# Attention wave 0 and its expert product: another order of casts, masks and products

## The chip, the cores and the metric

One core of one Trainium2 chip runs the whole program. The metric is the device time of one execution in microseconds. The engines named below are TensorE (PE, with its weight loads PEld), VectorE (DVE), ScalarE (ACT), GpSimd (POOL) and the DMA queue of SyncE (SP). Each works through its own instructions in the order in which they were written; they wait for each other only at semaphores.

## The reference

Linear attention with a decay per head, in blocks of 64 rows, and behind it an MLP on all tokens:

```python
# q, k, v: (4, 8, 768, 64) f32;  lam: (8,);  w_in: (512, 2048);  w_out: (2048, 512)
for b in range(nb):
    intra = einsum('bhic,bhjc->bhij', qb, kb) * Dmask
    intra = einsum('bhij,bhjd->bhid', intra, vb)
    inter = einsum('bhid,bhde->bhie', qb * lam_pow, kv_state)
    out[:, :, sl] = intra + inter
    kv_state = lam_block * kv_state + einsum('bhsd,bhse->bhde', kb * rev_pow, vb)
x = out.transpose(0, 2, 1, 3).reshape(3072, 512)
h = x @ w_in
y = (h / (1 + exp(-1.702 * h))) @ w_out
```

## The kernel before

The 768 rows of the four batches are cut into six waves (`w`) of 512 tokens; the MLP of a wave is done with its attention. Waves 0 and 1 (`w < ND`) take the first 256 rows of one batch as a chunk (`c` = 0, 1; wave 0 has batches 0 and 1, wave 1 has 2 and 3), with two neighbouring rows in one partition; waves 2 to 5 take 128 rows of all four batches. This case is about wave 0 and the beginning of wave 1.

Attention of one chunk in these waves:

- `load_one` brings k, q, v as f32 from DRAM (SP's queue; v of chunk 1 from POOL's queue). `do_cast` (lines 193 to 204) multiplies k or q by powers of the decay and writes bf16: for each half `g` of the heads two instructions of 128x256. Chunk 0's casts are on DVE, k of chunk 1 on POOL, q of chunk 1 on DVE.
- `turn_pe` (line 232) transposes the cast tile on PE into PSUM, and ACT or DVE copies it out (`kT`, `qT`). `cast_v` makes v bf16 (`v_sb`).
- `d_scores` (line 251) makes the scores in PSUM tiles `ps_s`, four tiles for a chunk in two calls, and multiplies each by the mask into `sm`: on DVE from PSUM, or, with `split`, every second tile by an ACT copy to SBUF and a DVE multiplication in place.
- `d_one`/`d_state` make the state `ps_kv` from the cast k and v, `d_keep` copies it out, `d_inter` multiplies q by the state, `d_out` multiplies `sm` by v into `ps_o`, and `d_x` copies that into `xT`, the MLP's input.
- `fill` issues matmuls on zeros into a bank that nobody reads.

The MLP's first product is `mlp1_half` (8 matmuls of 256 columns into one bank, then the GELU on ACT, line 416) and `mlp1` (4 of 512 columns, line 404). The weights come from POOL's queue: `load_w_in` in five chunks, the second of which holds the feature tiles 2 to 4, then `load_w_out` in four. Two DMAs are held back behind others by a tiny instruction that reads a tile: `gate_pool` and `gate_sync`.

The second product (`product`, line 448) is done by seven products of half size with sums of blocks (in the way of Strassen and Winograd), 16 matmuls of 256 columns each. The sums of w_out's blocks are `weight_sums` (steps `W`), those of the MLP's activations `g_sums` (steps `g`), both on DVE; sums of w_in's blocks, which later waves use, are `in_sums` (steps `I`). A bank in PSUM collects several products: by `CHAIN`, products 1, 6, 5 and 3 go to bank X, 2 to Q, 7 and 4 to V. `after_product` (line 471) takes a bank out after each product: ACT copies 1, 6 and 7 to `part`, and DVE adds a `part` to the bank to give a block of the output, `o_sb`, which SP stores; the block of product 2 is held back until step `o`.

The order is written by hand (`manual_schedule`, from line 639): calls for the start, then strings of steps, in which `p1a` is product 1 with the first part of its matmuls (`a`, `b`, `l`, `h` are parts), `P50` is product 5 for its first 128 tokens, `P51` for the second. Between the steps of wave 0 stand the pieces of wave 1's attention (`start`, `end`).

## Time and profile before

| | us |
|---|---|
| runs, median of 3 (lowest, highest) | 192.32 (192.29, 193.49) |
| the profiled execution | 192.84 |
| its span in the trace | 191.1 |
| steady part of a later wave, from one `ps_hX` group to the same one in the next wave (81.16 to 109.20) | 28.04 |

The profile's page gives the busy time of each engine, the chain of work that ended last and the costliest groups; the trace answers for single tiles and stretches. Two more rows are of use for the start: POOL's k casts of chunk 1 wait for the loads, and DVE is idle for 1.21 us before it copies the last `qT` of chunk 0 out.

```profile
9.07 0.42 DVE L218 COPY qT<-ps_t 128x512 bf16<-128x512 bf16 x1 [1.21 <-PE ps_t L238]
11.02 0.81 POOL L181 DMA_DIRECT2D w_in<-in_moe_w_in_dram  x1
16.02 0.43 DVE L267 TENSOR_TENSOR sm<-sm,mask_d 128x512 bf16<-128x512 bf16 x1
16.40 0.59 ACT L265 CAST sm<-ps_s 128x512 bf16<-128x512 f32 x1
```

A row is: start and length in us, engine, line, operation, what it writes and reads, the shapes, how many; in brackets the engine's idle time ahead of it and what ended it. Before the change the copy by ACT and the mask in place occur in chunk 1 of wave 0 alone.

### The profile page before, as it was taken

How to read it: one execution, taken by the hardware profiler on the slowest of the kernel's cores; microseconds unless marked ns; L12 is line 12 of the kernel's file. 1: busy time of each engine (PE TensorE's matmuls, PEld its weight loads, DVE VectorE, ACT ScalarE, POOL GpSimd, SP SyncE). 2: the span in 40 equal slices, each digit the busy share in tenths (PEclk: the TensorE clock that was granted, in tenths of full speed). 3: DMA queues.
4: the chain of work that ended last, by engine and by line, in shares of the span. 5: the costliest groups of instructions: out<-in, count | busy, mean ns of one | idle time of the engine just before them, and what ended most of it. 6: DMA issues, size and time to landing. Idle time of an engine off the chain costs nothing.

```text
span 191.1 us, 5544 instructions
## 1 busy us (share of the span) xinstructions
PE 184.6 (97%) x2297; PEld 152.2 (80%) x2297; DVE 156.3 (82%) x292; ACT 129.6 (68%) x242; POOL 53.7 (28%) x76
## 2 busy tenths in 40 slices
PE   7979999999999999999999999999999999999993
PEld 2557646888888888888888888888888888888882
DVE  1796699979978799879799879799789797888950
ACT  4948665257666986388896288885488876597611
POOL 5499000076495000195000294000492000000000
PEclk9999999999999999999999999999999999999999
DMA  4999999999997997868999555899565903300113
GB/s 144 313 290 197 204 200 209 321 310 229 215 241 178 214 247 165 207 163 139 208 243 216 187 153 127 197 241 230 175 152 122 209 4 113 110 3 0 54 59 110
DMA packets 89599, 33.91 MB, mean 177 GB/s; under 512 B 67430, under 2 KB 89446, under 8 KB 89574
## 3 DMA queue, kind: packets, MB, share of 16 engines
q1 hardware_dynamic: 84676, 28.84, 60.1%
q0 software_dynamic: 4896, 4.72, 14.5%
q8 instruction: 18, 0.29, 0.6%
q14 instruction: 7, 0.06, 0.1%
q10 hardware_dynamic: 2, 0.00, 0.0%
HBM read 27.26 MB, written 6.29 MB: 176 GB/s over the span
## 4 chain that ended last, share of the span: by engine, by line
PE 73%; DMA 11%; DVE 8%; POOL 2%; ACT 2%; issue 1%; SPq 0%; ACTq 0%
PE ps_X L461 19%; PE ps_hX L544 16%; PE ps_V L461 9%; PE ps_hV L544 8%; PE ps_Q L461 5%; DMA w_in<-in_moe_w_in_dram 5%; PE ps_hQ L544 4%; DVE w_in_t L520 3%; DMA kf<-in_k_dram 3%; DMA vf<-in_v_dram 3%; PE ps_h L414 2%; PE ps_s L335 2%; PE ps_o L390 2%; PE ps_fill L147 2%; POOL ks L202 1%; DVE sm L267 1%
## 5 line engine op out<-in xcount | busy, mean ns | idle before, releaser
L461 PEld LDWEIGHTS <-g_s 128*128 128x128 bf16 x384 | 37.0, 98 | 5.0
L563 ACT ACTIVATE g_sb<-h_sb 128x512 bf16<-128x512 f32 x54 | 32.6, 631 | 1.2 <-DVE h_sb L552 1.2
L544 PEld LDWEIGHTS <-w_in_t 128*128 128x128 bf16 x288 | 28.1, 98 | 3.4
L461 PEld LDWEIGHTS <-g_sb 128*128 128x128 bf16 x288 | 27.4, 98 | 4.1
L221 ACT COPY part<-ps_hX 128x512 f32<-128x512 f32 x32 | 18.3, 586 | 11.5 <-PE ps_hX L544 11.5
L461 PE MATMUL ps_X<-w_out_t,g_s 128*128 128x256 bf16 x192 | 23.1, 273 | 0.0
L544 PEld LDWEIGHTS <-w_in 128*128 128x128 bf16 x216 | 21.1, 98 | 2.5
L544 PE MATMUL ps_hX<-x_s,w_in_t 128*128 128x256 bf16 x144 | 21.6, 272 | 0.0
L441 DVE TENSOR_TENSOR g_s<-g_sb 128x1024 bf16<-128x1024 bf16 x24 | 16.3, 687 | 5.9 <-ACT g_sb L563 5.6
L634 POOL CAST behind_q<-x_s 1x1 f32<-1x1 bf16 x3 | 0.5, 174 | 60.3 <-DVE x_s L529 60.3
L209 POOL TENSOR_TENSOR qs<-qf,q_pow 128x512 bf16<-128x512 f32 x16 | 16.6, 1063 | 2.9 <-DMA qf<-in_q_dram 2.9
L209 POOL TENSOR_TENSOR ks<-kf,k_pow 128x512 bf16<-128x512 f32 x16 | 16.8, 1075 | 1.8 <-DMA kf<-in_k_dram 1.8
L474 ACT COPY part<-ps_X 128x512 f32<-128x512 f32 (+1 forms) x14 | 7.3, 522 | 13.0 <-PE ps_X L461 13.0
L218 DVE COPY part<-ps_hV 128x512 f32<-128x512 f32 x18 | 12.4, 688 | 3.7 <-PE ps_hV L544 3.7
L552 DVE TENSOR_TENSOR h_sb<-part,ps_hX 128x512 f32<-128x512 f32 x18 | 12.3, 681 | 2.7 <-PE ps_hX L544 2.7
L552 DVE TENSOR_TENSOR h_sb<-part,ps_hV 128x512 f32<-128x512 f32 x18 | 12.3, 684 | 1.0 <-PE ps_hV L544 1.0
L461 PE MATMUL ps_X<-w_out,g_sb 128*128 128x256 bf16 x96 | 12.6, 273 | 0.0
L461 PE MATMUL ps_Q<-w_out,g_sb 128*128 128x256 bf16 x96 | 12.5, 273 | 0.0
L552 DVE TENSOR_TENSOR h_sb<-part,ps_hQ 128x512 f32<-128x512 f32 x18 | 12.2, 679 | 0.0
L461 PE MATMUL ps_V<-w_out_t,g_sb 128*128 128x256 bf16 x96 | 12.0, 273 | 0.0
L563 ACT ACTIVATE g_sb<-ps_hX 128x512 bf16<-128x512 f32 x18 | 10.6, 588 | 1.8 <-PE ps_hX L544 1.8
L461 PE MATMUL ps_V<-w_out_t,g_s 128*128 128x256 bf16 x96 | 11.6, 273 | 0.0
(111 smaller groups left out, 362.3 us busy)
## 6 DMA issues: line engine op xcount, KB each, us to landing
kf<-in_k_dram SPq DMA_DIRECT2D x10, 512.0 KB, 6.4
qf<-in_q_dram SPq DMA_DIRECT2D x10, 512.0 KB, 7.2
vf<-in_v_dram SPq DMA_DIRECT2D x10, 512.0 KB, 6.0
out_dram<-o_sb SPq DMA_DIRECT2D x24, 128.0 KB, 2.4
out_dram<-o_sb SPq DMA_DIRECT2D x12, 256.0 KB, 2.7
w_out<-in_moe_w_out_dram POOLq DMA_DIRECT2D x4, 512.0 KB, 14.1
kf<-in_k_dram SPq DMA_DIRECT2D x4, 256.0 KB, 3.1
qf<-in_q_dram SPq DMA_DIRECT2D x4, 256.0 KB, 5.2
```

What stands on the lines that cost most here:

```text
L147: nc.tensor.matmul(fill_ps[0], zero[:, 0:P], zero, start=True, stop=True)
L209: eng.tensor_tensor(x.rearrange("p b (r i j d) -> p j (b r) i d", i=2, j=2, d=D)[:, j], f.rearrange("p h (a d) -> p (h a) d", a=2).rearran ...
L218: nc.vector.tensor_copy(out, in_)
L221: nc.scalar.copy(out, in_)
L335: nc.tensor.matmul(s2[h][:, b, :], kT[hs, (b % 2) * NP + p, :], qT[hs, (b % 2) * NP + p, :], start=True, stop=True)
L441: nc.vector.tensor_tensor(o, x, y, op=f)
L461: nc.tensor.matmul(bank[:, t], x[:, m, t * P : (t + 1) * P], y, start=(n in (1, 2, 7) and t == ts[0] * last and m == 0), stop=(m == FFC // ...
L474: nc.scalar.copy(part[w, n, t.start][:, t], bank[:, t])
L520: nc.vector.tensor_tensor(o, x, y, op=SUB)
L544: nc.tensor.matmul(bank[:, u], z[:, kc], y[:, kc], start=(n in (1, 2, 7) and u + kc == 0), stop=(kc == 1), skip_group_check=True)
L552: nc.vector.tensor_tensor(h, h_part[w, g, {2: 1, 5: 7, 4: 6}[n]], bank, op=ADD)
L563: nc.scalar.activation(g_of[w][:, a : b + 1 : b - a, 256 * i : 256 * i + 256], bank, GELU)
```

## The change

In wave 0 and the beginning of wave 1:

- `load_w_in(1)` is issued from POOL's queue ahead of the k casts of chunk 1 instead of between their halves.
- `do_cast` writes a tile in another layout, `[P, NP, 2, P]`, and does a half in one instruction of 128x512. `turn_pe` and `d_state` read that layout.
- The masks leave `d_scores` for `d_masks`. In wave 0, chunks 0 and 1, the two score calls come first, then the masks of the first tile of each call on DVE, then those of the second tiles by an ACT copy and DVE in place.
- Two `fill` matmuls are left out. The transposes of chunk 1, the second state product and the `xT` copies stand in another order, one transposed half is copied out by ACT instead of DVE, and `cast_v(0, 1)` stands behind `mlp1_half(0, 0, 0)` instead of ahead of it.
- In wave 0's second product, product 4 has a bank of its own (Z) and stands in part between 7 and the last parts of 1, 2 and 7. DVE adds product 6 to product 7's `part`; product 5 is copied out by ACT into a `part`, and its sum for the output comes with a new step `u`. Product 3 comes earlier, directly behind product 5 and `d_even`. `start` is now `scores`, `d_one`, `d_keep` and `d_even` at places of their own.

```diff
     def do_cast(w, c, nm, eng, g=None):
         if g in (None, 0):
-            cast[w, c, nm] = work.tile([P, 2, HD], bf16, tag=f"{nm}s{c}", bufs={"k": 2, "q": 1}[nm], name=f"{nm}s")
+            cast[w, c, nm] = work.tile([P, NP, 2, P] if w < ND else [P, 2, HD], bf16, tag=f"{nm}s{c}",
+                                       bufs={"k": 2, "q": 1}[nm], name=f"{nm}s")
...
-                for j in range(2):
-                    h = slice(4 * R + 2 * j, 4 * R + 2 * j + 2)
-                    eng.tensor_tensor(x.rearrange("p a (r i j d) -> p r j i a d", i=2, j=2, d=D)[:, R, j],
-                                      f[:, h].rearrange("p i (a d) -> p i a d", a=2),
-                                      pw[:, h].unsqueeze(3).to_broadcast([P, 2, 2, D]), op=MUL)
+                h = slice(4 * R, 4 * R + 4)
+                eng.tensor_tensor(x[:, 2 * R : 2 * R + 2].rearrange("p i a (j d) -> p j (i a) d", j=2),
+                                  f[:, h].rearrange("p (j i) (a d) -> p j (i a) d", j=2, a=2),
+                                  pw[:, h].rearrange("p (j i) a -> p j (i a)", j=2).unsqueeze(3).to_broadcast([P, 2, 4, D]),
+                                  op=MUL)
...
-        for h in range(2):
+        masked[w, c, pp] = s2
+
+    def d_masks(w, c, pp, hh=(0, 1), split=()):
+        for h in hh:
             sm = work.tile([P, 2, 2, P], bf16, tag="sm", bufs=8, name="sm")
-            flat = s2[h].rearrange("p (i a) s -> p i (a s)", i=2)
-            if split and h:
+            flat = masked[w, c, pp][h].rearrange("p (i a) s -> p i (a s)", i=2)
+            if h in split:
                 nc.scalar.copy(sm.rearrange("p i a s -> p i (a s)"), flat)
...
+        own = w == 0 and n == 4
+        if own and ms[0] == 0:
+            blocks[w, "Z", key] = acc("ps_Z", shape=[P, 2, 256])
+        bank = blocks[w, "Z" if own else CHAIN[n], key]
...
         if n in (1, 6, 7):
             part[w, n, t.start] = op.tile([P, 2, 256], f32, tag="part", bufs=6, name="part")
-            nc.scalar.copy(part[w, n, t.start][:, t], bank[:, t])
+            if n == 6 and w == 0:
+                nc.vector.tensor_tensor(part[w, n, 0], part[w, 7, 0], bank, op=ADD)
+            else:
+                nc.scalar.copy(part[w, n, t.start][:, t], bank[:, t])
...
+        if n == 5 and w == 0 and (w, 5) not in part:
+            part[w, 5] = op.tile([P, 2, 256], f32, tag="part", bufs=6, name="part")
+            nc.scalar.copy(part[w, 5], bank)
+            c22[w] = partial(after_product, w, n, part[w, 5], t)
+            return
...
         load_one(0, 1, "v", v)
+        load_w_in(1)
         cast_v(0, 0, (act_copy, act_copy))
         d_scores(0, 0, 0)
         d_scores(0, 0, 1)
-        fill(3)
+        for h in range(2):
+            for pp in range(2):
+                d_masks(0, 0, pp, (h,), (1,))
+        fill(2)
         do_cast(0, 1, "k", nc.gpsimd, 0)
-        load_w_in(1)
         do_cast(0, 1, "k", nc.gpsimd, 1)
...
-        d_state(0, 0, states[0, 0], Z)
         do_cast(0, 1, "q", nc.vector, 0)
         do_cast(0, 1, "q", nc.vector, 1)
-        d_x(0, 0, 0, oa, act_copy)
+        turn_pe(0, 1, "k", act_copy, 1)
         turn_pe(0, 1, "q", act_copy, 0)
         d_inter(0, 0, oz, 0, False)
-        turn_pe(0, 1, "k", dve_copy, 1)
         turn_pe(0, 1, "q", dve_copy, 1)
+        d_state(0, 0, states[0, 0], Z)
+        d_x(0, 0, 0, oa, act_copy)
         d_x(0, 0, 1, oz, act_copy)
-        fill(1, "a")
-        d_scores(0, 1, 0, True)
+        d_scores(0, 1, 0)
+        d_scores(0, 1, 1)
+        for h in range(2):
+            for pp in range(2):
+                d_masks(0, 1, pp, (h,), (1,))
+        mlp1_half(0, 0, 0)
         cast_v(0, 1, (act_copy, dve_copy))
...
-        d_scores(0, 1, 1, True)
-        mlp1_half(0, 0, 0)
         d_one(0, 1)
...
-        steps(0, "p1a gh3 p2a W23124 p1b p2b gh12 p7l W3312 p1h p2h p7h")
+        steps(0, "p1a gh3 gh1 p2a W23124 p1b p2b gh2 gh4 p7l p4l W33124 p1h p2h p7h")
         do_cast(1, 0, "k", nc.vector)
-        steps(0, "p6l p6h p4a")
         do_cast(1, 0, "q", nc.vector)
+        steps(0, "p6l")
         turn_pe(1, 0, "k", act_copy)
-        steps(0, "p4b W34 gh4 o")
+        steps(0, "p6h")
+        turn_pe(1, 0, "q", act_copy)
+        steps(0, "p4h o")
         load(2, "kq")
         cast_v(1, 0)
         do_cast(1, 1, "k", nc.gpsimd)
-        turn_pe(1, 0, "q", act_copy)
-        steps(0, "p4h P50")
-        start(1, 0)
+        steps(0, "P50")
+        scores(1, 0)
+        d_one(1, 0)
+        d_keep(1, 0)
+        steps(0, "P51")
+        d_even(1, 0, "mm")
         cast_v(1, 1, (act_copy, act_copy))
         do_cast(1, 1, "q", nc.gpsimd)
-        steps(0, "P51")
+        steps(0, "P30")
         turn_pe(1, 1, "k", act_copy)
         end(1, 0)
-        steps(0, "P30 I2")
+        steps(0, "u P31 I2")
         turn_pe(1, 1, "q", act_copy)
...
             if i == 1:
-                steps(0, "P31")
-                start(1, 1)
+                scores(1, 1)
+                d_even(1, 1)
```

## The prediction, made before the changed kernel ran

> **What bounds the kernel now.** I read the page first (busy time, chain), then busy time by stretches, then the timelines of the two stretches whose instructions the change moves. From the page, busy time by engine and the chain's shares:
>
> ```profile
> PE 184.6 (97%) x2297; PEld 152.2 (80%) x2297; DVE 156.3 (82%) x292; ACT 129.6 (68%) x242; POOL 53.7 (28%) x76
> PE 73%; DMA 11%; DVE 8%; POOL 2%; ACT 2%; issue 1%; SPq 0%; ACTq 0%
> ```
>
> PE sets the time. The busy time by stretches (start:end, length, then each engine's busy time) says where PE still waits:
>
> ```profile
> 10.00:15.00 5.00, 4.03 (x100) 2.59 (x103) 4.62 (x10) 2.59 (x6) 4.98 (x8) 1.00 1.24 272
> 44.00:48.00 4.00, 3.84 (x100) 3.41 (x99) 3.97 (x9) 3.28 (x7) 2.24 (x5) 1.00 0.89 205
> 81.00:109.00 28.00, 28.00 (x354) 24.47 (x352) 24.57 (x44) 20.77 (x38) 8.11 (x10) 1.00 0.87 199
> ```
>
> From 53.37 us, where 40 first-MLP matmuls start, the order of every engine is as it was and PE does not wait. So the question is when PE reaches those 40. Before them lie the start (to 18.72, where 24 such matmuls begin; from there to 31.76 PE streams) and wave 0's second product with wave 1's attention (31.76 to 53.37).
>
> The start, from its timeline (start, length, engine, line, what):
>
> ```profile
> 9.49 2.48 DVE L267 TENSOR_TENSOR sm<-ps_s,mask_d 128x512 bf16<-128x512 f32 x4
> 9.89 1.18 POOL L202 TENSOR_TENSOR ks<-kf,kd_pow 128x256 bf16<-128x256 f32 x2 [0.86 <-ACT v_sb L221]
> 11.85 1.39 POOL L202 TENSOR_TENSOR ks<-kf,kd_pow 128x256 bf16<-128x256 f32 x2
> 11.89 2.30 DVE L202 TENSOR_TENSOR qs<-qf,qd_pow 128x256 bf16<-128x256 f32 x4
> 15.73 1.05 PE L414 MATMUL ps_h<-xT,w_in 128*128 128x256 bf16 x8
> 15.88 0.62 ACT L221 CAST v_sb<-vf 128x512 bf16<-128x512 f32 x1
> 16.71 0.47 PE L279 MATMUL ps_kv<-v_sb,ks 64*64 64x64 bf16 x13
> 16.88 0.61 ACT L416 ACTIVATE g_sb<-ps_h 128x512 bf16<-128x512 f32 x1
> 18.72 2.84 PE L414 MATMUL ps_h<-xT,w_in 128*128 128x256 bf16 x24
> ```
>
> DVE's four masks end at 11.97 and then its q casts run until 14.19, slowed while POOL casts k. The state product at 16.71 follows the 8 matmuls without a wait, since v_sb was cast before the GELU. The later stretch:
>
> ```profile
> 45.47 0.68 DVE L485 TENSOR_TENSOR o_sb<-part,ps_X 128x512 f32<-128x512 f32 x1
> 46.37 1.05 PE L461 MATMUL ps_X<-w_out,g_s 128*128 128x256 bf16 x8
> 47.52 0.42 DVE L520 TENSOR_TENSOR w_in_t<-w_in,w_in_t 128x512 bf16<-128x512 bf16 x1
> 47.78 2.27 POOL L209 TENSOR_TENSOR ks<-kf,k_pow 128x512 bf16<-128x512 f32 x2 [1.76 <-DMA kf<-in_k_dram]
> 47.87 1.27 DVE L520 TENSOR_TENSOR w_in_t<-w_in 128x512 bf16<-128x512 bf16 x1
> ```
>
> The same sum of two SBUF tensors takes 0.42 alone and 1.27 beside a POOL cast. Masks read from PSUM are not slowed: four took 2.48 from 9.49, beside POOL's casts.
>
> **The start, step by step.** Unit costs: a 128x512 op on f32 takes DVE 0.68, one every 0.60 (the four masks); a 128x256 0.42, one every 0.34 (four k casts at 4.63 in 1.43); an ACT copy of 128x512 0.58, one every 0.49; eight 256-column matmuls 0.87, eight transposes 0.44.
>
> 1. *Casts by halves.* A pair of 256s is 0.76, one 512 I put at the PSUM row's 0.68; the bounds are 0.42 (the bf16 512 row) and 0.76. The first k half gates the transposes at 5.45, behind which PE runs without a wait to 8.96, so everything there comes 0.07 earlier (0 to 0.34). POOL: a 512 cast is 1.07 (L209, mean of the page) against 1.18 for the pair.
> 2. *w_in's second chunk first.* POOL waited 0.86 before its first k cast; the issue takes 0.81 (up to 0.95) and fits there, so that cast starts at 9.87 as before. Cover gone, it would cost 0.9 on the k chain. The chunk's landing (5.9 us after an issue at 11.02) gates nothing: PE reads it at 18.72. That it slows the q loads would cost only what exceeds 0.44, the slack until step 4. The later weights are issued 1.1 earlier, but the DMA slices stand at 9 there, so I move no landing: gain nothing.
> 3. *Masks, split with ACT.* DVE masks two tiles from PSUM (9.42, 10.02 to 10.70). ACT copies the other two behind its v_sb copies: 9.70 to 10.29, 10.19 to 10.78. DVE then masks these in place in SBUF, 0.42 each: 11.37 if alone, 0.6 earlier than 11.97. But POOL casts k from 9.87 to about 12.1, and now they meet. In the row at 47.87 DVE ends 0.28 after POOL's cast (47.78+1.08=48.86; 49.14). So the first ends at 10.93+0.28=11.21, the second behind POOL's next cast (10.91+1.22=12.13) at 12.41: 0.44 later than before. The Trainium skill, SBUF — State Buffer, section Who interferes with whom, says that a tensor_tensor with two SBUF inputs and a GpSimd op that reads SBUF shut each other out for a whole instruction. By that rule the masks end at this 12.41; read as a rate (1.27 each) they would end at 13.08 and the start at +1.30.
> 4. *q casts of chunk 1* follow with POOL done: 12.33 to 13.02 and to 13.62 (were 13.52 and 14.19).
> 5. *PE and ACT behind it.* Last output matmuls at 12.47, k transpose 12.72, q transposes 13.08 and 13.68. ACT's queue is now k, q, and both x copies: 13.16, 13.64, 14.12, 14.60 to 15.19. So the 8 matmuls start at 15.26, 0.47 earlier than 15.73. The state product that moved behind the transposes fills waiting time.
> 6. *The v_sb copy goes behind the GELU on ACT.* It stood ahead. GELU starts about 1.10 after the 8 matmuls start: 16.36; v_sb 16.85 to 17.47; the state product, in PE's order behind the 8, starts at 17.53 (was 16.71), its copy 0.48 later at 18.01 to 18.38, the read of it 18.54 (was 17.91). Everything behind keeps its distance: the 24 matmuls start at 19.35. **+0.63.** Its ends: +0.09 if the masks don't meet POOL (8 matmuls at 14.73), +1.30 if the slowing is a rate.
> 7. *Two fewer fillers* (0.21 each) lay in waiting time: nothing. If they keep the clock up, see the rivals.
>
> **The second product.** 8. Up to the fifth product PE issues the same 80 matmuls of 256 columns in w_out's products, 16 of them product 4's, and 16 transposes: 41.35 against 41.39. The weight sums these want end 0.8 or more before them; w_out's last chunk is wanted later than before. 9. DVE adds product 6 onto product 7 (0.68, ACT's copy less) and finishes product 4 and 2 by about 42.8, when the scores of wave 1 are out: nothing. If a bank for the scores waits for product 4's sum: up to 0.2. 10. *Product 3 directly behind product 5*, in the same bank: it must wait until ACT has copied the bank out (matmul end +0.17, copy 0.58, hand-overs 0.10), with 4 small matmuls (0.06) between: **0.74 of idle PE**, and all of PE's order behind it. Before, DVE read that bank at 45.47 while PE did other work. 11. The q transpose of chunk 1 moves 0.87 closer to its scores, behind an extra ACT copy: scores wait about 0.44. The masks after it: w_in sums no longer beside POOL if the next k load lands later (its issue stands behind two more output stores), so only 0.46 before the last quarter of the output product.
> 12. What goes away: PE's idle time between 31.76 and 53.37. Those 21.61 hold 136 matmuls (14.82), 32 transposes (1.76) and about 3.0 of small ones, so 2.0 idle. After: 0.08+0.74+0.15+0.44+0.46+0.2 is 2.1. **+0.1** (from −1.2, if 10 and 11 are covered, to +1.05, if the w_in sums do meet POOL once or twice, 0.85 each, less slack).
>
> Sum +0.73. The profiled execution took 192.84 (span 191.1, 1.7 around it); the median of the runs is 192.32, 0.5 less. The step is a length of PE time, so 192.32+0.73: **193.0 us**.
>
> **Rivals.** *It gains* (0.27): masks clear of POOL (+0.09) and steps 10 and 11 covered (−1.2): 191.2. For it: every queue got shorter in front of PE; against it: ACT's order shows the copy between products 5 and 3. Beyond 1% it comes only if nearly all the 2.0 idle goes (0.09): 190.3. *The w_in sums meet the next POOL casts* (0.20): the next k load lands while they run, as in the row at 47.87; +0.95 with 1.70 of slowing, less the wait for the scores: 194.0; with step 3 as a rate too, above 194.3 (0.07). *The clock drops* (0.08): step 6 leaves PE idle from 16.13 to 17.53, 1.4 us, with two fillers gone; the longest such wait before is 0.88 at 12.70, and there the clock held. At half the clock (fillers at 5.85 came every 0.43, those at 9.90 every 0.21, though the granted clock's row reads 9 from the first slice) the 24 matmuls cost 2.6 more: 195.6. It decides from the idle length at which the clock falls, which the trace doesn't show. The Trainium skill, TensorE: Matmul & The Clock Gate, Part 1, puts it at about 3.4 us idle; by that rule nothing would drop here. *The change doesn't do what it says*: the chunk issued earlier lands no earlier, which is step 2 already.
>
> **The numbers.** Forecast 193.0 (0.45, own range 192.3 to 193.8). Tellable from no change is about 1%, 1.9 us: below 190.4 or above 194.2. Faster 0.09 from the first rival, say 0.10; slower 0.07 and 0.08, so 0.15; same 0.75. The range 190.9 to 194.4 leaves out the best of the gains (0.1) and the clock with the worst of the sums (0.1).
>
> **What would show it.** Two in-place masks ending 0.28 behind POOL's k casts near 11.2 and 12.4; an idle PE of over 1 us between 8 first-MLP matmuls and the state product, released by ACT's v_sb; the 24 at about 19.3; PE idle about 0.7 before product 3, released by ACT; the 40 at about 54.1. It is wrong if the masks end before 11.5, if v_sb is not what the state product waits for, if product 3 starts without a wait, or if anything after the 40 moves by itself.

## The result, and the profile after

| | before | changed |
|---|---|---|
| runs, median (lowest, highest), us | 192.78 (192.29, 193.49) | 195.26 (194.40, 198.63) |
| the profiled execution, us | 192.84 | 194.94 |
| its span, us | 191.1 | 193.2 |

The ratio of changed to before is 1.0109, 95% interval 1.0062 to 1.0157: slower by about 1.1%, where 193.0 was forecast with a range up to 194.4. Runs that were disturbed (the 198.63 among them, and the profiled executions of three kernels below) are left out of the ratios and of the readings; without the 198.63 the changed kernel's median is 194.94. The page of the changed kernel: busy time, the granted clock in 40 slices, the shares of the chain.

```profile
PE 183.9 (95%) x2295; PEld 152.2 (79%) x2295; DVE 153.6 (79%) x282; ACT 130.8 (68%) x245; POOL 53.5 (28%) x70
...
PEclk9979999999999999999999999999999999999999
...
PE 85%; DVE 5%; DMA 2%; ACT 2%; POOL 2%; issue 1%; SPq 1%; ACTq 0%; DVEq 0%
```

PE is busy for less of a longer span, and the clock's row has a 7 in its third slice that the kernel before has not. Its busy time by stretches, in the columns of the prediction:

```profile
8.22:11.63 3.41, 1.88 (x50) 1.07 (x50) 3.08 (x5) 2.42 (x6) 3.41 (x5) 1.00 1.21 291
11.63:15.05 3.42, 3.38 (x56) 2.65 (x56) 2.41 (x3) 1.73 (x5) 3.42 (x5) 0.50 1.18 261
10.00:15.00 5.00, 3.52 (x66) 2.68 (x61) 3.90 (x5) 2.65 (x7) 5.00 (x7) 0.66 1.22 253
44.00:48.00 4.00, 3.56 (x78) 2.92 (x76) 3.07 (x6) 2.33 (x6) 2.33 (x3) 1.00 0.42 102
83.10:111.10 28.00, 28.00 (x354) 24.47 (x352) 24.57 (x44) 20.77 (x38) 8.11 (x10) 1.00 0.84 194
```

PE's row falls from 4.03 to 3.52 between 10 and 15 us and from 3.84 to 3.56 between 44 and 48, and is 28.00 of 28.00 later on, as before. From 11.63 to 15.05 PE had half the clock. The rows of the two stretches that answer to those shown ahead of the change follow; here and below, a group that runs past the end of a view is counted only up to there, so the 24 matmuls show as x5, x12 or the like:

```profile
7.08 0.70 POOL L651 COPY behind_q<-qf 1x1 f32<-1x1 f32 x1 [3.71 <-DMA qf<-in_q_dram]
10.34 2.46 POOL L202 TENSOR_TENSOR ks<-kf,kd_pow 128x512 bf16<-128x512 f32 x2
...
10.24 1.65 DVE L271 TENSOR_TENSOR sm<-sm,mask_d 128x512 bf16<-128x512 bf16 x2
11.82 1.52 DVE L202 TENSOR_TENSOR qs<-qf,qd_pow 128x512 bf16<-128x512 f32 x1
13.68 0.69 DVE L202 TENSOR_TENSOR qs<-qf,qd_pow 128x512 bf16<-128x512 f32 x1 [0.33 <-DMA qf<-in_q_dram]
...
16.17 1.03 PE L418 MATMUL ps_h<-xT,w_in 128*128 128x256 bf16 x8
18.39 0.38 PE L283 MATMUL ps_kv<-v_sb,ks 64*64 64x64 bf16 x13 [1.19 <-ACT v_sb L222]
20.13 0.72 PE L418 MATMUL ps_h<-xT,w_in 128*128 128x256 bf16 x5
...
40.31 2.11 DVE L202 TENSOR_TENSOR qs<-qf,qd_pow 128x512 bf16<-128x512 f32 x2
42.48 0.40 PE L239 MATMUL ps_t<-ident,qs 128*128 128x128 bf16 x4 [0.18 <-DVE qs L202]
46.66 1.03 PE L468 MATMUL ps_X<-w_out,g_s 128*128 128x256 bf16 x8 [0.44 <-ACT seen L310]
51.87 0.64 PE L260 MATMUL ps_s<-qT,kT 64*64 64x128 bf16 x32 [0.34 <-ACT qT L222]
```

POOL's k casts start at 10.34 instead of 9.89; one in-place mask and the first q cast are stretched beside them; the last q cast waits for its load; PE waits 1.19 for `v_sb`; later it waits 0.44 ahead of product 3 and 0.34 ahead of the scores of chunk 1.

Where the 2.10 between the two profiled executions lie, from PE's rows (us):

| stretch of PE | before | changed | difference | forecast |
|---|---|---|---|---|
| to the 8 first-MLP matmuls | 15.73 | 16.17 | +0.44 | −0.47 |
| from the 8 to the 24 | 2.99 | 3.96 | +0.97 | +1.10 |
| from the 24 to product 1 | 13.04 | 13.04 | 0 | 0 |
| from product 1 to the 40 | 21.61 | 22.30 | +0.69 | +0.1 |
| from the 40 to the end | 137.8 | 137.8 | 0 | 0 |

This compares one execution with one other. The first kernel's start, unedited, is also in three of the kernels below, and there the 8 start at 14.90, 15.22 and 15.70 and the 24 at 18.12, 18.21 and 18.68, against 15.73 and 18.72 in the profile shown ahead of the change. That profile is thus the latest of four, by up to 0.83 at the 8.

### The profile page after: what moved, and what is told of

Read it like the earlier page. It is cut to its first block, busy times and chain, and to the rows that moved or that the text cites. A ratio compares the mean times of both kernels' runs of the same rounds, so it can differ in the third digit from the quotient of the medians.

```text
span 193.2 us, 5527 instructions
## 1 busy us (share of the span) xinstructions
PE 183.9 (95%) x2295; PEld 152.2 (79%) x2295; DVE 153.6 (79%) x282; ACT 130.8 (68%) x245; POOL 53.5 (28%) x70
## 4 chain that ended last, share of the span: by engine, by line
PE 85%; DVE 5%; DMA 2%; ACT 2%; POOL 2%; issue 1%; SPq 1%; ACTq 0%; DVEq 0%
PE ps_X L468 20%; PE ps_hX L559 16%; PE ps_V L468 9%; PE ps_hV L559 8%; PE ps_h L406 5%; PE ps_h L418 5%; PE ps_Q L468 5%; PE ps_hQ L559 4%; DMA qf<-in_q_dram 2%; PE ps_s L339 2%; PE ps_o L394 2%; DVE w_out_t L432 2%; PE ps_t L239 1%; PE ps_o L320 1%; PE ps_o L381 1%; DVE qs L202 1%
## 5 line engine op out<-in xcount | busy, mean ns | idle before, releaser
L210 POOL TENSOR_TENSOR ks<-kf,k_pow 128x512 bf16<-128x512 f32 x16 | 16.3, 1040 | 5.9 <-DMA kf<-in_k_dram 5.9
L484 ACT COPY part<-ps_X 128x512 f32<-128x512 f32 (+1 forms) x13 | 6.7, 517 | 13.2 <-PE ps_X L468 13.2
L468 PE MATMUL ps_X<-w_out,g_s 128*128 128x256 bf16 x96 | 11.6, 272 | 0.4 <-ACT seen L310 0.4
```

What stands on the lines that cost most here:

```text
L210: eng.tensor_tensor(x.rearrange("p b (r i j d) -> p j (b r) i d", i=2, j=2, d=D)[:, j], f.rearrange("p h (a d) -> p (h a) d", a=2).rearran ...
L468: nc.tensor.matmul(bank[:, t], x[:, m, t * P : (t + 1) * P], y, start=((n in (1, 2, 7) or own) and t == ts[0] * last and m == 0), stop=(m ...
L484: nc.scalar.copy(part[w, n, t.start][:, t], bank[:, t])
```

## The experiments

Each ratio is against the first kernel's runs on the same chip, with its 95% interval. "The 8", "the 24" and "the 40" are the starts of those groups of first-MLP matmuls, as in the prediction. Where a row has no times, none are read from its trace.

| kernel | ratio | the 8 | 8 to 24 | product 1 to the 40 |
|---|---|---|---|---|
| new product alone | 1.0044 (1.0015 to 1.0072) | 14.90 | 3.22 | 22.79 |
| new start alone | 1.0064 (1.0037 to 1.0092) | 15.29 | 3.96 | 21.61 |
| v cast first | 1.0141 (1.0116 to 1.0167) | 16.11 | 4.08 | 22.31 |
| w_in between the casts | 1.0135 (1.0108 to 1.0163) | 15.64 | 3.96 | 23.16 |
| the changed kernel again | 1.0143 (1.0104 to 1.0182) | | | |
| v first, 8 fillers | 1.0097 (1.0062 to 1.0131) | 15.97 | 3.60 | 22.31 |
| product 3 later | 1.0036 (1.0008 to 1.0064) | 15.70 | 2.98 | 23.10 |
| new start mended | 1.0035 (1.0018 to 1.0052) | 15.54 | 4.01 | 21.38 |
| v cast before the masks | 0.9998 (0.9971 to 1.0025) | 14.73 | 3.20 | 21.37 |
| w_in back | 0.9990 (0.9961 to 1.0018) | | | |
| transposes later | 1.0004 (0.9974 to 1.0034) | 15.22 | 2.99 | 21.82 |
| all mended | 1.0016 (0.9984 to 1.0048) | 15.59 | 3.10 | 21.82 |
| 8 fillers alone | 1.0136 (1.0087 to 1.0185) | 15.97 | 3.97 | 23.14 |
| w_in after the casts | 1.0024 (0.9992 to 1.0056) | 14.84 | 3.55 | 21.37 |
| v cast before the masks, again | 1.0016 (0.9989 to 1.0043) | | | |

### The change in two halves

New product alone: the first kernel's start with the changed second product (its order of steps, product 4's own bank, product 6 summed by DVE, product 5 copied out by ACT).

```diff
-        steps(0, "p1a gh3 p2a W23124 p1b p2b gh12 p7l W3312 p1h p2h p7h")
+        steps(0, "p1a gh3 gh1 p2a W23124 p1b p2b gh2 gh4 p7l p4l W33124 p1h p2h p7h")
...
-        steps(0, "p4h P50")
-        start(1, 0)
+        steps(0, "P50")
+        scores(1, 0)
+        d_one(1, 0)
+        d_keep(1, 0)
+        steps(0, "P51")
+        d_even(1, 0, "mm")
...
+        steps(0, "P30")
```

> The start as before, with the changed second product. Theory A (both parts lose, as the trace of the changed kernel reads: 1.4 us up to the 24 first-MLP matmuls, 0.7 us from there to the 40): the 24 start at 18.7 as before, the 40 at about 54.0 (before 53.37), time 0.3 to 0.7 us above before. Rival B (all of the loss comes from the start, and the product part only looked slower because the GELUs that feed DVE's sums came late): the 40 at 53.4 or earlier, time within 0.2 us of before or below it.

New start alone: the changed start with the first kernel's second product, that is the rest of the change's lines.

> The changed start with the second product as before. Theory A: the 24 start at about 20.1 and the 40 at 53.4+1.4=54.8, time 1.4 us above before. Rival B: the 24 at 20.1 and the 40 at 55.4, time 2.1 above before. If the start's lateness is taken up later by waits that were there anyway, the 40 come before 54.3.

Measured 1.0044 and 1.0064, +0.85 and +1.23 us; together 1.0108, the changed kernel's 1.0109. Both halves lose. That their losses simply add is not shown: measured once more, the changed kernel gave 1.0143, and the intervals are wide enough for both. The new start's rows:

```profile
6.82 0.27 POOL L638 COPY behind_q<-qf 1x1 f32<-1x1 f32 x1 [3.44 <-DMA qf<-in_q_dram]
9.64 2.08 POOL L202 TENSOR_TENSOR ks<-kf,kd_pow 128x512 bf16<-128x512 f32 x2
...
10.09 2.26 DVE L271 TENSOR_TENSOR sm<-sm,mask_d 128x512 bf16<-128x512 bf16 x2
12.27 1.28 DVE L202 TENSOR_TENSOR qs<-qf,qd_pow 128x512 bf16<-128x512 f32 x2
...
15.29 1.03 PE L418 MATMUL ps_h<-xT,w_in 128*128 128x256 bf16 x8 [0.34 <-ACT xT L222]
17.52 0.38 PE L283 MATMUL ps_kv<-v_sb,ks 64*64 64x64 bf16 x13 [1.19 <-ACT v_sb L222]
19.25 1.53 PE L418 MATMUL ps_h<-xT,w_in 128*128 128x256 bf16 x12
```

In this execution the start ends each step within 0.1 of what the prediction worked out: last mask 12.35 (12.41), q casts to 13.55 (13.62), the 8 at 15.29 (15.26), the state product at 17.52 (17.53), the 24 at 19.25 (19.35). For the masks that is in part luck. The durations of the two in-place masks (shortest, median, longest, in ns), here and then in the changed kernel, tell two different stories:

```profile
L271 DVE TENSOR_TENSOR sm<-sm,mask_d x2: 409/1166/1924, 10.1 to 11.9; 128x512 bf16<-128x512 bf16 x2
L271 DVE TENSOR_TENSOR sm<-sm,mask_d x2: 470/818/1165, 10.2 to 10.7; 128x512 bf16<-128x512 bf16 x2
```

The prediction had one mask end behind each of POOL's two k casts. In the new start alone both casts (to 11.72) went ahead of the first mask, which took 1.92 and ended 0.29 behind the second cast; the second mask took 0.41. In the changed kernel the first mask came ahead of POOL's casts and took 0.47, and the second ended 0.29 behind POOL's first cast, at 11.90.

The +0.53 at the 24 against the first profile is less than the 1.23 of the times, and the starts differ from one execution to the next: over four profiles the first kernel's start reaches the 24 at 18.12 to 18.72, and over three the changed start (this one, the changed kernel's, and that of 8 fillers alone below) at 19.25 to 20.13.

For the product, PE's busy time between product 1 and the 40, first in the kernel before, then with the new product alone:

```profile
31.76:53.37 21.61, 21.26 (x377) 18.38 (x376) 19.18 (x37) 11.98 (x22) 9.10 (x13) 1.00 1.04 266
```

```profile
31.16:53.95 22.79, 21.51 (x377) 18.34 (x375) 19.43 (x42) 11.89 (x22) 8.39 (x12) 1.00 0.99 250
```

PE idled for 0.35 before and for 1.28 now; the other 0.25 of the 1.18 is in PE's busy time, whose ends are modelled. The prediction had 2.0 of idle there to win back. With the new product alone the idle stands in four places, of which the timeline shows three; the fourth is the 0.34 ahead of the scores of chunk 1:

```profile
39.63 0.40 PE L238 MATMUL ps_t<-ident,ks 128*128 128x128 bf16 x4 [0.23 <-DVE ks L202]
40.98 0.40 PE L238 MATMUL ps_t<-ident,qs 128*128 128x128 bf16 x4 [0.27 <-DVE qs L202]
45.15 1.03 PE L464 MATMUL ps_X<-w_out,g_s 128*128 128x256 bf16 x8 [0.44 <-ACT part L489]
```

### The order of v_sb, and the clock

v cast first, in the changed kernel:

```diff
-        mlp1_half(0, 0, 0)
         cast_v(0, 1, (act_copy, dve_copy))
+        mlp1_half(0, 0, 0)
```

> The changed kernel with the cast of v (chunk 1) ahead of the first 8 MLP matmuls and their GELU, as it stood before. Theory A: PE's 1.2 us of waiting between the 8 matmuls and the state product (17.2 to 18.4) goes, the 24 start 0.8 to 1.1 us earlier (19.0 to 19.3), time 0.8 to 1.1 below the changed kernel. Rival C (the state product would wait for something else, the late q cast or its masks): the 24 stay within 0.2 us of 20.1.

w_in between the casts, in the changed kernel:

```diff
         load_one(0, 1, "v", v)
-        load_w_in(1)
...
         do_cast(0, 1, "k", nc.gpsimd, 0)
+        load_w_in(1)
         do_cast(0, 1, "k", nc.gpsimd, 1)
```

> The changed kernel with the second chunk of w_in issued between the two k casts again. Rival D (the early issue is what costs: it holds POOL's first k cast to 10.34 and lets weight packets in ahead of the last q half, which landed at 13.65 instead of 12.02): the first k cast starts at 9.6, the last q half lands before 12.6, the 24 start 0.7 to 1.1 us earlier. Theory A without D: the k cast comes 0.7 earlier but the second one, behind the issue, no earlier; the q half lands at 13.6 as in the changed kernel, and the 24 start within 0.3 us of 20.1.

Measured 1.0141 and 1.0135: neither is below the changed kernel. In the first, the runs behind the ratio had a mean clock of 0.989 to 0.991, and the trace shows why the new place of `v_sb` brought nothing:

```profile
14.28:17.69 3.41, 3.41 (x60) 2.50 (x60) 2.32 (x6) 2.90 (x6) 3.41 (x6) 0.50 1.25 198
```

```profile
16.11 1.80 PE L418 MATMUL ps_h<-xT,w_in 128*128 128x256 bf16 x8
...
18.48 0.35 PE L283 MATMUL ps_kv<-v_sb,ks 64*64 64x64 bf16 x11 [0.43 <-DVE v_sb L219]
```

The 8 matmuls ran at half the clock, 1.80 instead of 1.03, and when they were done DVE's half of `v_sb` was late. In the second, the first k cast started at 9.20, the last q half landed at 11.34 and the 24 came at 19.60, 0.53 earlier than in the changed kernel's profile. But PE waited 1.04 for DVE's q cast in the second product, beside POOL's casts, against 0.18 in the changed kernel's profile. That meeting varies: of five profiles with the changed kernel's casts and second product, two have the 1.04 (this one and 8 fillers alone) and three 0.18 to 0.20.

The changed kernel was run again for more times, without an edit.

> The changed kernel as it is, for a second profile and more times. Theory A (the loss is the sum of three: about +0.9 between the 8 first-MLP matmuls and the 24 behind them, about +0.7 in the second product, and a start that differs from execution to execution by when the last half of q lands and by whether the clock drops for 3.4 us): the 24 start between 19.2 and 20.2, 3.9 to 4.0 behind the 8, the 40 start 22.2 to 23.1 behind product 1, and the ratio is 1.009 to 1.013. Rival B (half the clock is the main loss): where the profile shows clock 1.0 the 24 start at 18.7 to 19.0 and the time is below 194.

It gave 1.0143; the runs with a mean clock of 0.998 or more were 194.65 to 195.59, so full clock doesn't bring it below 194 and rival B of the expectation falls. No times are read from its profile, so the starts that theory A named were not tested.

v first, 8 fillers: the edit of v cast first, and

```diff
-        fill(2)
+        fill(8)
```

> The changed kernel with the v_sb casts ahead of the 8 first-MLP matmuls and eight fillers instead of two in the wait for POOL's k cast, so that PE isn't idle there. Theory A (the v_sb copy behind the GELU costs about 0.8, and in the kernel with only that order turned the dropped clock took it back: 8 matmuls in 1.80 instead of 1.03): clock 0.997 or more in nearly all runs, the 24 start 3.1 to 3.3 behind the 8, and the ratio falls to 1.005 to 1.009. Rival B (the order of ACT isn't what holds PE; the masks on DVE or the transposed k are): the distance stays at 3.9 or more and the ratio at 1.011 or more.

The clock was 1.000 in five of six runs, and the 8 took their full speed again. From the 8 to the 24 it is 3.60, between the two expectations, and PE still waits 0.46 and 0.19 for `v_sb`. The median was 194.44, ratio 1.0097: in the trace, part of what the order of `v_sb` costs is back (3.60 for 3.96), but the interval overlaps the changed kernel's, so that the times alone don't show it.

8 fillers alone: the changed kernel with that one line.

> The changed kernel with eight fillers instead of two and nothing else. Theory A (the dropped clock is a smaller part of the loss, since PE mostly waits while it is down): clock 0.997 or more in nearly all runs, the 24 start 3.9 to 4.0 behind the 8, ratio 1.008 to 1.012. Rival B (the clock is what makes the changed start lose more than the 0.53 that its undisturbed profile showed): ratio 1.004 to 1.007.

The clock was 0.999 or 1.000 in all six runs, and the ratio 1.0136, above both expectations. The dropped clock is not what makes the changed start lose. The profile of this run serves for another thing, since its start ran at full clock and its last q half landed at 11.60, nearly as early as in the new start alone (11.31):

```profile
7.07 0.70 POOL L651 COPY behind_q<-qf 1x1 f32<-1x1 f32 x1 [3.69 <-DMA qf<-in_q_dram]
10.33 2.08 POOL L202 TENSOR_TENSOR ks<-kf,kd_pow 128x512 bf16<-128x512 f32 x2
...
10.71 2.33 DVE L271 TENSOR_TENSOR sm<-sm,mask_d 128x512 bf16<-128x512 bf16 x2
...
...
15.97 1.03 PE L418 MATMUL ps_h<-xT,w_in 128*128 128x256 bf16 x8 [0.34 <-ACT xT L222]
...
19.94 1.31 PE L418 MATMUL ps_h<-xT,w_in 128*128 128x256 bf16 x10
```

Row by row it is the new start alone, 0.68 to 0.69 later: k casts 10.33 for 9.64, last mask 13.04 for 12.35, last q cast 14.24 for 13.55, the 8 at 15.97 for 15.29, the 24 at 19.94 for 19.25. The shift arises in POOL's first row: the 1x1 copy that gates POOL's queue started 0.25 later and took 0.70 instead of 0.27. DVE's second q cast of chunk 0, now 0.69 long, ran from 7.04 to 7.73, and the copy ended with it. Then come three issues back to back (0.95, 0.91, 0.78) and the k casts, with no idle time on POOL that could take the shift in. In the first kernel's profile POOL was idle for 0.86 there, because k's load for that cast landed late, at 9.75. But that idle time was not the rule either. The same unedited start in new product alone and in transposes later:

```profile
6.74 1.04 POOL L647 COPY behind_q<-qf 1x1 f32<-1x1 f32 x1 [3.36 <-DMA qf<-in_q_dram]
9.58 1.21 POOL L202 TENSOR_TENSOR ks<-kf,kd_pow 128x256 bf16<-128x256 f32 x2
...
9.38 1.18 POOL L202 TENSOR_TENSOR ks<-kf,kd_pow 128x256 bf16<-128x256 f32 x2
```

There k landed at 8.90 and 9.24, and POOL was idle for 0.00 and 0.10 ahead of the k casts; in product 3 later for 0.14. The first of these rows also shows the copy at 1.04 beside the old, shorter casts, so that the longer casts are not needed for a late copy.

### Mending the start

New start mended: on new start alone, all four masks of chunk 0 from PSUM, `v_sb` ahead of the 8, eight fillers.

```diff
-                d_masks(0, 0, pp, (h,), (1,))
-        fill(2)
+                d_masks(0, 0, pp, (h,))
+        fill(8)
...
-        mlp1_half(0, 0, 0)
         cast_v(0, 1, (act_copy, dve_copy))
+        mlp1_half(0, 0, 0)
```

> The changed start with the first kernel's second product, and in the start three things undone: all four masks of chunk 0 read PSUM on DVE (no ACT copies, nothing masked in place), the v_sb casts stand ahead of the 8 matmuls, eight fillers instead of two. What is left of the change is the casts in one instruction and w_in's second chunk ahead of the k casts. Theory A (the start's loss is the lock of in-place masks with POOL's casts and the v_sb copy behind the GELU, and the rest of the edit is worth 0 to 0.5): the masks end at 11.3 to 12.0 with none over 0.75, q casts end by 13.5, the 24 start at 17.8 to 18.6, ratio 0.997 to 1.001. Rival B (the halves in one instruction, slower when they meet POOL, or w_in's earlier bytes ahead of q's cost the start): the 24 start at 19.0 or later, ratio 1.004 or more.

It gave 1.0035, between the two expectations. The masks ended at 11.39, but the first q cast then met POOL's second k cast (1.64 long), and the second waited until 13.53 for its load. From the 8 to the 24 it stayed 4.01:

```profile
17.84 0.35 PE L283 MATMUL ps_kv<-v_sb,ks 64*64 64x64 bf16 x11 [0.64 <-DVE v_sb L219]
```

ACT's half of `v_sb` was there in time. DVE's half stood behind four masks in DVE's queue; in the first kernel it stood between the second and the third. So one more step:

```diff
+        cast_v(0, 1, (act_copy, dve_copy))
         for h in range(2):
             for pp in range(2):
                 d_masks(0, 1, pp, (h,), (1,))
-        cast_v(0, 1, (act_copy, dve_copy))
         mlp1_half(0, 0, 0)
```

> The mended start with the two v_sb casts moved further, ahead of chunk 1's four masks on DVE and ACT. Theory A (not only ACT's half of v_sb stood behind the GELU, DVE's half stood behind four masks, and moving the casts just ahead of the 8 matmuls left that half to end PE's wait, 0.64 in the run before): PE doesn't wait for v_sb, the state product starts within 1.1 of the 8 matmuls, the 24 start 3.1 to 3.4 behind the 8 instead of 4.0, the ratio falls by 0.003 or so to 1.000 to 1.001. Rival B (the output matmuls then wait as long for the masks, which end 0.5 later): the distance stays at 3.7 or more and the ratio at 1.003.

It gave 0.9998. The rows:

```profile
11.27 1.62 DVE L202 TENSOR_TENSOR qs<-qf,qd_pow 128x512 bf16<-128x512 f32 x2
...
14.73 1.03 PE L418 MATMUL ps_h<-xT,w_in 128*128 128x256 bf16 x8 [0.34 <-ACT xT L222]
15.69 0.38 PE L283 MATMUL ps_kv<-v_sb,ks 64*64 64x64 bf16 x12
...
17.93 2.30 PE L418 MATMUL ps_h<-xT,w_in 128*128 128x256 bf16 x19
```

POOL's k casts stand here at 9.65 and 10.65, within 0.01 of new start alone, so the two traces can be laid side by side: without the in-place masks the q casts end at 12.89 instead of 13.55 and the 8 start 0.56 earlier; with `v_sb` ahead of the masks the state product doesn't wait, and the 24 follow the 8 after 3.20 instead of 3.96, another 0.76. Together that is 1.32. By the ratios the last step can't be told (1.0035 ahead of it, 0.9998 and, measured again below, 1.0016 with it, with overlapping intervals), so it too rests on the traces. The masks were never undone alone, so the 0.56 rests on these two traces; the six more fillers, which changed too, had won no time in 8 fillers alone.

Two places of w_in's second chunk were tried on this kernel, between the k casts and behind them:

```diff
         load_one(0, 1, "v", v)
-        load_w_in(1)
...
         do_cast(0, 1, "k", nc.gpsimd, 0)
+        load_w_in(1)
         do_cast(0, 1, "k", nc.gpsimd, 1)
```

> The same with w_in's second chunk issued between POOL's k casts, as in the first kernel. Theory A (the chunk issued early takes transfer time from q: its last half landed at 13.4 to 13.65 in four of six profiles with the early issue, at 11.2 to 12.0 in all without): the last q half lands by 12.1, no q cast waits for it, the 8 matmuls start 14.7 to 15.3, ratio 0.997 to 1.000. Rival B (the landing of q differs from run to run for other reasons, and what is won there goes to the second k cast, 0.8 later behind the issue): the 8 start at 15.4 or later, ratio not below the run with the early issue.

```diff
         load_one(0, 1, "v", v)
-        load_w_in(1)
...
         do_cast(0, 1, "k", nc.gpsimd, 1)
+        load_w_in(1)
```

> The mended start (masks from PSUM, v_sb casts ahead of chunk 1's masks, eight fillers, casts in one instruction, the first kernel's second product) with w_in's second chunk issued behind both of POOL's k casts. Theory A (the early chunk's bytes hold back the last q half in most executions): the last q half lands by 12.1, the k casts start as early as with the early issue (9.6 to 10.3), the 24 start at 17.8 to 18.3, and the time is 0.5 to 1.0 below that of the run with the early issue beside it, ratio 0.994 to 0.998. Rival B (the landing of q isn't set by that chunk): time within 0.3 of the run beside it.

> The same with the early issue, as measured before, for a comparison on the same chip and a second profile. Theory A: the last q half lands at 13.4 to 13.7 where POOL's first w_in issue starts at 7.4 or later, and by 12.1 where it starts at about 7.0; in the late case the 24 start 0.6 to 1.2 later than 17.93. Rival B: the landing doesn't follow POOL's issues. Ratio 0.998 to 1.001 by both.

The ratios are 0.9990 beside 0.9998, and 1.0024 beside 1.0016: the place of that issue doesn't move the time by an amount these runs can tell, and the theory that the chunk's bytes hold q back falls as an explanation of the loss. The last q half did land at 13.5 to 13.65 in three profiles with the early issue (the changed kernel, v first with 8 fillers, new start mended), but at 11.3 to 11.9 in four others with it. In the seven profiles read here without the early issue it landed by 12.02 each time, so that the early issue may still be one condition of the late landing. What decides it is open.

### Mending the second product

Product 3 later: new product alone, with the k transposes between products 5 and 3.

```diff
-        steps(0, "P30")
         turn_pe(1, 1, "k", act_copy)
+        steps(0, "P30")
         end(1, 0)
```

> The first kernel's start with the changed second product, but PE's k transposes of chunk 1 put between product 5 and product 3. Theory A (product 3 directly behind product 5 waits 0.44 for ACT's read of the bank, and this wait is part of the 0.85 that the new product costs alone): PE's idle before product 3 falls from 0.44 to under 0.1, the 40 start 0.3 to 0.45 nearer to product 1 than with the new product alone, ratio 1.001 to 1.003. Rival B (PE would wait for the same ACT queue a step later, at the masks or the outputs): the 40 don't move by more than 0.15, ratio 1.003 to 1.006.

PE no longer waited ahead of product 3, but in that execution `w_out` landed 0.34 late for product 1 and the two waits on DVE's casts were 0.27 each; the 40 came 23.10 behind product 1, and 1.0036 doesn't tell the theories apart. Transposes later, on top of it:

```diff
-        steps(0, "p6l")
+        steps(0, "p6l p6h")
         turn_pe(1, 0, "k", act_copy)
-        steps(0, "p6h")
-        turn_pe(1, 0, "q", act_copy)
         steps(0, "p4h o")
+        turn_pe(1, 0, "q", act_copy)
```

> The first kernel's start with the changed second product, with product 3 behind the k transposes of chunk 1 and the transposes of wave 1's first k and q each one product half later. Theory A (the new product loses by three waits that the order makes, on DVE's casts 0.27 and 0.27, on ACT's read of the bank 0.44, on the q transpose's copy 0.34, of which the first three go): PE's idle between product 1 and the 40 falls from 1.2 to 0.4 to 0.7, the 40 start 22.0 to 22.3 behind product 1, ratio 1.000 to 1.002. Rival B (the scores take the wait over, since they stand one product behind the transposes and the ACT copy takes 1.0): the 40 start 22.7 or more behind product 1, ratio 1.003 or more.

It gave 1.0004. PE's busy time in the same stretch, then the two waits that are left, of which the last is as before this edit:

```profile
31.25:53.07 21.82, 21.22 (x377) 18.43 (x376) 18.36 (x39) 11.70 (x22) 8.39 (x12) 1.00 0.97 249
```

```profile
42.17 0.64 PE L259 MATMUL ps_s<-qT,kT 64*64 64x128 bf16 x32 [0.26 <-ACT qT L221]
...
49.48 0.64 PE L259 MATMUL ps_s<-qT,kT 64*64 64x128 bf16 x32 [0.34 <-ACT qT L221]
```

Idle fell from 1.28 in new product alone to 0.60. The ratio fell with it, but its interval still overlaps that of new product alone, so the gain is shown by the trace and not by the times alone. All mended is the changed kernel with the mended start (w_in between the casts) and this product.

> The changed kernel with all of it: masks of chunk 0 from PSUM, eight fillers, v_sb casts ahead of chunk 1's masks, w_in's second chunk between the k casts, product 3 and the transposes of the second product later. Theory A (the causes add up): start as in the run with w_in back, second product as in the run with the transposes later, clock 1.0, ratio 0.998 to 1.002, so the changed kernel's loss is accounted for. Rival B (something else of the change costs, as the larger casts against POOL's in the second product): ratio 1.004 or more.

It gave 1.0016, with 1 inside the interval and the changed kernel's 1.0109 far outside. The loss is accounted for by the order of `v_sb`, the masks, and the transposes and product 3, together with the fillers and the place of w_in's chunk, which by the runs above won no time of their own. None of the mended kernels is faster than the first by an amount that could be told.

## Why the prediction missed

The direction was right and the size too small by 1.37 (2.10 against 0.73 between the profiled executions): +0.91 ahead of the 8, −0.13 behind them, +0.59 in the second product. By the times of the two halves the misses are 0.60 in the start (1.23 for 0.63) and 0.75 in the second product (0.85 for 0.1). The base of the forecast was low as well: 192.32 was the median of three runs, and with a fourth it is 192.78.

- *Step 1, casts by halves.* The unit costs held: 0.68 to 0.69 on DVE, 1.07 to 1.08 a POOL cast that isn't held up. Missed was that DVE's q casts stop POOL's gating copy: it ended with the second of them, 0.70 long instead of 0.38 in the first kernel's profile. That is not the longer casts alone, since it took 1.04 beside the old ones in new product alone.
- *Step 2, w_in's second chunk first.* **This step failed.** The cover, POOL's 0.86 of idle time, was taken for certain, with 0.05 to spare over the issue. It was there in one of four profiles of that start; in the other three it was 0.00 to 0.14. With the issue in that place any delay ahead of it goes to the k casts undiminished: 9.64 in one execution, 10.33 and 10.34 in two others; between the first two of these the whole start shifts by the same 0.69. The prediction named the case (cover gone) and left it out of the sum. What the early issue itself costs in time is not shown: with it moved back the changed kernel gave 1.0135, and the mended start was no faster. The slack of 0.44 for q loads was exceeded too, in the changed kernel's profile: the last q cast waited for its load until 13.68.
- *Steps 3 and 4, masks and q casts.* Right in kind, and right in size partly by luck. A mask that meets POOL's casts does end 0.29 behind one of them, where 0.28 was worked out, but not in the order that was forecast: the 12.35 of the new start alone (for 12.41) came from one mask waiting for both casts, and in the changed kernel the masks ended at 11.90. The rule cited there from the Trainium skill, SBUF — State Buffer, Who interferes with whom, that each shuts the other out for a whole instruction, agrees with those rows; as a rate they would have ended at 13.08. The price of masking in place was larger than the 0.44 of the mask: beside a start with masks from PSUM, 0.66 at the q casts.
- *Step 5.* Right to 0.03 in the new start alone; 0.91 late in the changed kernel's profile. There the last q cast ended 0.75 late (14.37 for 13.62): POOL's first k cast came 0.47 late, and DVE then waited 0.33 for the last q half to land. The half clock lies in the rest. These runs don't part the three.
- *Step 6, v_sb behind the GELU.* Right as to place and size: 3.96 from the 8 to the 24 where 4.09 was worked out, and an idle PE of 1.19, released by ACT's `v_sb`, where 1.4 was. Half of the mechanism was missed. DVE's half of `v_sb` stands behind four masks, so undoing ACT's order alone left PE waiting, 0.64 in the mended start.
- *Step 7.* Two fillers less cost nothing measurable: six more brought the clock back and no time.
- *Steps 8 and 9.* No wait on the bank of product 4 or on a weight sum shows up in the profiles read here.
- *Step 10.* Right as to the wait and what ends it, ACT's copy of the bank, but PE idles 0.44 behind the four small matmuls where 0.74 was worked out. (The terms given there, 0.17, 0.58 and 0.10 less 0.06, sum to 0.79.)
- *Step 11.* Right in kind: 0.34 for the 0.44 worked out.
- *Step 12.* **This step failed, and it is the larger plain error.** It set 2.1 of new idle time against 2.0 of old, the latter by subtracting unit costs, with 3.0 for all the small matmuls. The busy row of just that stretch has PE busy for 21.26 of 21.61, so 0.35 was idle and the small ones took 21.26−14.82−1.76=4.7. The new waits were then almost all loss. They too were put too high, 2.1 for a measured 1.28 with the new product alone, and this hid half of the error: no wait of 0.46 ahead of the output product and none of 0.2 on a bank came, and two terms (0.08 and 0.15) have no row. The waits on DVE's casts ahead of the transposes weren't seen: 0.23 and 0.27 with the new product alone, up to 1.04 where the longer casts met POOL's.
- *The rivals.* The w_in sums did not meet POOL's casts, 0.42 each from 50.48. The clock did drop, in the changed kernel's profile and by the mean clock (0.991) in one of the four later runs behind its ratio. In the profile it came behind the wait for the k casts, not behind step 6, and it decides nothing: at full clock the ratio was 1.0136.

## What to carry to other kernels

Read idle time from the busy row of the very stretch; a difference of unit costs turned 0.35 us into 2.0. A copy on two engines has two queues: move it ahead of what it gates on both. When an issue is put into an engine's idle time, ask whether that time is there in every execution: here it was there in one profile of four.

## What the runs showed of the hardware

- *The clock falls after a window that is only partly idle.* In the changed kernel the profile has half the clock from 11.63 to 15.05, 3.42 long, and in v cast first from 14.28 to 17.69, 3.41 long. The 3.41 ahead of the fall held 1.53 of idle PE in the first (8.22 to 11.63, busy 1.88) and 1.25 in the second (10.87 to 14.28). With 8 fillers alone, a window with 1.29 idle (15.89 to 19.30) was followed by full clock. So idle time alone gives no threshold here. (The rows of the last two windows stand below.) The Trainium skill, TensorE: Matmul & The Clock Gate, Part 1, has free-running windows of 3413 ns, which agrees with the lengths, and the slow clock after at least one idle window; the trace shows it after a window in which PE was busy for more than half the time.
- *A 1x1 copy on POOL lasts until a DVE cast beside it ends.* In all profiles it ran beside DVE's q casts, which have two SBUF inputs, and ended 0.04 behind the end of one of them. It took 0.27 in the new start alone (6.82 to 7.09, the first cast ending at 7.05) and 0.70 in 8 fillers alone, where it started at 7.07, just behind the start of the second cast at 7.04. So a start 0.25 later became an end 0.69 later.
- *A DVE mask can wait for two POOL casts in a row.* In place in SBUF it took 0.41 when it met none and 1.92 in the new start alone, where it ended 0.29 behind the second of POOL's casts. In w_in between the casts the first mask started at 10.51, when POOL's first cast had ended (10.25) and the second not begun (11.01), and it too ended 0.29 behind the second, at 12.36; why is open.

The window ahead of the fall in v cast first, and the one of 8 fillers alone that no fall followed:

```profile
10.87:14.28 3.41, 2.16 (x54) 1.50 (x55) 3.25 (x4) 1.84 (x6) 3.41 (x4) 1.00 1.22 275
15.89:19.30 3.41, 2.12 (x65) 1.71 (x66) 1.93 (x5) 2.74 (x7) 2.06 (x4) 1.00 1.22 198
```
